# Two second-product tiles in a row: first products 3, 2, 0, 2 between the tiles of the expert stage

## The chip, the cores and the metric

The kernel runs on one core of a Trainium2 chip. The metric is device time of the whole program in microseconds (us); each time below is the median of three runs. TensorE (PE) does the matrix products, VectorE (DVE), ScalarE (ACT) and GpSimd (POOL) everything else; weights and tokens come and go by DMA, issued from SyncE (SP).

## What is computed

1152 tokens of 512 columns pass through three layers: a two-part attention (the first 170 us, with the first steps of the next layer beside it), a layer of 8 experts with a gate `P` that is balanced in 8 rounds (called the balancing below), and a dense layer with softplus.

```python
x = attention(q, k, v)                      # (1152, 512)
P = balanced(exp(x @ w_gate))               # 8 rounds of row and column sums
out = 0
for e in range(8):
    out += P[:, e:e+1] * (maximum(x @ w1[e], 0) @ w2[e])
h = out @ w_in
return softplus(h) @ w_out                  # d_ff = 2048
```

## The kernel before

**Tiling.** The tokens stand in two groups, s = 0 (512 tokens, four tiles of 128) and s = 1 (640 tokens, five tiles). The dense layer with its 2048 hidden columns is treated as two further "experts", e = 8 and 9, whose weights are brought into the same form earlier. An expert's hidden columns come in four pieces p. One *step* n of the list `steps` is one expert, one piece and one token group; there are 80, numbered from 0, and steps 4 to 79 are issued by the loop at the end of the kernel with an order fixed by hand on PE, ACT, DVE and POOL.

**First products.** `first(n)` makes the hidden values of step n. A fast matrix multiplication replaces eight products of half size by seven (`OPS = 7`). Each is six matmuls at L841: two halves of the contraction, times three pairs of high and low parts of the operands, with 256 columns for s = 0 and 320 for s = 1. They come in the order 4, 0, 2, 5, 1, 3, 6 and share three accumulators of PSUM, `m0`, `m1`, `m2`. Product 4 goes to an accumulator `m4` in the listings, and a copy `t1` of it is taken by ACT (`kept`, L853). Product 0 goes to `m0`, copied as `t5`. Product 2 is *added into the accumulator of product 4*, so its first matmul must wait until `t1` has been copied; the sum is copied as `u2`, and only then product 1 is written over it. Product 5 has the third accumulator. DVE adds the pieces (`combine`, L860): `c11` after product 5, `c22` after product 1, `c12` after product 3; `c21` is product 6 itself.

**Hidden values.** For each of the four pieces a job `hidden` is put into the planner. In the expert layer it is a ReLU on ACT (L778) and a subtraction on DVE (L780), giving high and low parts. In the dense layer it is a softplus chain of nine instructions: ACT Abs (L788), ACT Exp (L790), DVE +1 (L799), DVE error (L801), ACT Ln (L803), POOL subtraction (L805), DVE maximum and sum (L808), ACT cast (L810), DVE subtraction (L812). In the dense layer `c21` is also copied by ACT (L853) first.

**Second products.** `second` multiplies one tile of 128 tokens of hidden values with the second weights: six matmuls of 512 columns at L929. `weigh` adds the result to the output rows on DVE.

**The order on PE.** While step n makes its second products, tile by tile, the first products of a later step (usually n + 2) are issued between the tiles; `ahead` says which. Before each tile a share of what is left is issued, rounded up:

```python
for m, i in enumerate(tiles):
    for _ in range(-(-left // (len(tiles) - m))):
        next(products)
        left -= 1
```

With seven products this gives 2, 2, 2, 1 before the four tiles of an s = 0 step and 2, 2, 1, 1, 1 before the five of an s = 1 step. I call the tiles A, B, C, D and E in the order in which they are issued. During steps 4 to 8 one piece of the balancing follows every tile but the first; every second piece has a small matmul (L727) that needs what DVE made in the piece before.

**The order on the other engines.** The class `Order` is a planner with assumed durations. Every product and tile moves its clock on (`advance`), and it puts each waiting job instruction on its engine where it expects the engine free. ACT, DVE and POOL work their lists off in that order, so an instruction whose input is late holds up all those behind it. Where a step needs something of a job, `until` issues that job, and others with it. Besides the hidden chains the planner issues the splitting of weights, of the dense layer's weights (L351 to L375), and of the tokens between the layers (`operands`: L437 and L441 on DVE, L439 on ACT).

Of the kernel before, what the change touches and what calls it, by code (L numbers as in the profile page):

```python
# [20 lines left out]
def attention_moe_mlp(ctx: ExitStack, tc: tile.TileContext, q, k, v, w_gate, w1, w2, w_in, w_out, out):  # L21
# [3 lines left out]
    E, _, FF = w1.shape  # L25
# [26 lines left out]
    OPS = 7  # L52
# [654 lines left out]
    def sinkhorn():  # L707
        mt = spare[0][:, HALF[1] : HALF[1] + P]
        nc.tensor.transpose(mt[:1], m1, ident)
        m2 = const.tile([1, 1], F32, name="m2")  # L710
        nc.vector.tensor_reduce(m2, mt[:1], axis=AX.X, op=ALU.max)
        yield
        mb = spare[0][:, HALF[1] : HALF[1] + 1]
        nc.tensor.matmul(mb, ones[:1, :], m2, start=True, stop=True)
        m3 = const.tile([P, 1], F32, name="m3")
        nc.vector.tensor_copy(m3, mb)
        nc.vector.tensor_scalar(prf, prf, m3, None, op0=ALU.subtract)
        nc.scalar.activation(prf, prf, AF.Exp)
        for it in range(8):
            rs = const.tile([P, NTT, 1], F32, tag="grs", name="grs")  # L720
            nc.vector.tensor_reduce(rs, pr, axis=AX.X, op=ALU.add)
            nc.vector.tensor_scalar(rs, rs, EPS, None, op0=ALU.add)
            nc.vector.reciprocal(rs, rs)
            nc.vector.tensor_tensor(pr, pr, rs.to_broadcast([P, NTT, E]), op=ALU.mult)
            yield
            cp = spare[0][:, HALF[1] : HALF[1] + NTT * E]
            nc.tensor.matmul(cp, ones, prf, start=True, stop=True)  # L727
            cs = const.tile([P, 1, E], F32, tag="gcs", name="gcs")
            nc.vector.tensor_reduce(
                cs, cp.rearrange("p (t e) -> p e t", e=E), axis=AX.X, op=ALU.add  # L730
            )
            nc.vector.tensor_scalar(cs, cs, EPS, None, op0=ALU.add)
            nc.vector.reciprocal(cs, cs)
            nc.vector.scalar_tensor_tensor(
                out=pr, in0=pr, scalar=float(NT) / E, in1=cs.to_broadcast([P, NTT, E]), op0=ALU.mult, op1=ALU.mult
            )
            yield
# [14 lines left out]
    for e, g, s, p in steps:  # L752
        m = e * NP + p
# [161 lines left out]
    def outputs(s):  # L915
        return [bank(tag, "yps") for tag in ("at", "at", "at", "at", "y")[: len(TILES[s])]]

    def second(n, hh, hl, i, y, start, stop):
        s = steps[n][2]
        order_.force(fetching[uses[n], 1])  # L920
        for j, job in making[n]:
            if j * HALF[s] < (i + 1) * P and (j + 1) * HALF[s] > i * P:
                order_.force(job)
        wh, wl = weights[uses[n]][1]
        tok = slice(i * P, (i + 1) * P)
        m = 0
        for f in range(2):
            for a, b in ((hh, wh), (hh, wl), (hl, wh)):
                nc.tensor.matmul(y, a[:, f, tok], b[:, f, :], start=(start and m == 0), stop=(stop and m == 5))  # L929
                m += 1  # L930
        order_.advance(6 * 0.231)
# [6 lines left out]
    def scale_rows(t):  # L938
        yield "POOL", 0.95, order_.free.get("DVE", 0.0)
        nc.gpsimd.tensor_tensor(acc[t], acc[t], pr[:, t, 0:1].to_broadcast([P, DM]), op=ALU.mult)  # L940
# [3 lines left out]
    def weigh(e, s, i, y):  # L944
        t, e = TILES[s][i], min(e, E)
        once = (e, t) not in seen
        seen.add((e, t))
        if e in (0, E) and once:
            acc[t] = rows[s].tile([P, DM], F32, tag="row", name="acc")
            order_.did("DVE" if i % 2 else "ACT", 0.65)  # L950
            (nc.vector.tensor_copy if i % 2 else nc.scalar.copy)(acc[t], y)
        elif e in (0, E):
            order_.did("DVE", 0.745)
            nc.vector.tensor_tensor(acc[t], y, acc[t], op=ALU.add)
        else:
            if e == 1 and once:
                order_.force(scaled[t])
            order_.did("DVE", 0.745)
            nc.vector.scalar_tensor_tensor(  # L959
                out=acc[t], in0=y, scalar=pr[:, t, e : e + 1], in1=acc[t], op0=ALU.mult, op1=ALU.add,  # L960
            )

    def again(s, banks):

        if not s:
            order_.force(converting[0])
        if s:
            xf = [pair("xf2") for _ in range(2)]
        else:
            xf = [x.tile([P, 2, 2 * HALF[s]], F32, tag="raw", name="xf2") for x in rawp]  # L970
        for i, t in enumerate(TILES[s]):
            tp = bank(banks, "tp")
            for kk in range(KD):
                nc.tensor.transpose(tp[:, kk * P : (kk + 1) * P], acc[t][:, kk * P : (kk + 1) * P], ident)
            tpv = tp.rearrange("p (a k c) -> p a k c", a=2, k=2)
            order_.advance(0.43)
            for kk in range(2):
                order_.did("ACT", 0.38)
                nc.scalar.copy(xf[kk][:, :, i * P : (i + 1) * P], tpv[:, :, kk])
            yield  # L980
        for kk in range(2):
            split[s].append(order_.add(operands(s, kk, xf[kk], ORDER, [nc.vector], order_.free.get("ACT", 0.0)), 2, TURN))
# [7 lines left out]
    def used(n):  # L990
        f = uses[n]
        if final[f] == n and f + 3 < len(fetches):
            fetch_second(f + 3, fetches[f + 3])
# [93 lines left out]
    last = ends[E, 1]  # L1087
    ahead[last - 1], ahead[last] = [], [last + 1, last + 2]
    balance, pending = sinkhorn(), None

    def conversions():
        loaded = yield from load(pieces[0], 0.0)
        for piece, upcoming in zip(pieces, pieces[1:] + [None]):
            loaded = yield from convert(piece, *loaded, upcoming)
# [5 lines left out]
    def leading(ns):  # L1100
        for n in ns:
            if steps[n][0] == E and n == (turned[1] if steps[n][2] else ends[E, 1] + 1):
                for _ in pending:
                    pass
            yield from lead(n)

    engines = {mybir.EngineType.PE, mybir.EngineType.Activation, mybir.EngineType.DVE, mybir.EngineType.Pool}
    with tc.manual_schedule(engines=engines):
        order_.on = True
        order_.free.clear()  # L1110
        order_.read.clear()
        for n in range(BESIDE, len(steps)):
            if n == CV:
                converting.append(order_.add(conversions(), 2))
            e, g, s, p = steps[n]
            if begins[n]:
                ys = outputs(s)
            hs = ready.pop(n)
            products = leading(ahead.get(n, []))
            left = OPS * len(ahead.get(n, []))  # L1120
            if n == ends[E - 1, 0]:

                left -= len(TILES[0]) - 1

            half = [i for i in range(len(ys)) if (i + 1) * P > HALF[s]]
            half = half[1:] + half[:1] if HALF[s] % P else half
            tiles = half + [i for i in range(len(ys)) if i not in half]
            for m, i in enumerate(tiles):
                for _ in range(-(-left // (len(tiles) - m))):
                    next(products)  # L1130
                    left -= 1
                if pending:
                    next(pending, None)
                second(n, *hs, i, ys[i], begins[n], stops[n])
                if stops[n]:
                    weigh(e, s, i, ys[i])
                if m and balance:
                    order_.did("DVE", 0.6)
                    if next(balance, True):
                        balance = None  # L1140
                        for t in range(NTT):
                            scaled[t] = order_.add(scale_rows(t))
                if pending:
                    next(pending, None)
            if n == ends[E - 1, 0]:
                pending = again(0, "at")
                for _ in TILES[0]:
                    next(pending)
                    next(products, None)
            for _ in products:  # L1150
                pass
            used(n)
            if n == ends[E - 1, 1]:
                pending = again(1, "y")
            elif n in (ends[NE - 1, 0], ends[NE - 1, 1]):
                for t in TILES[s]:
                    nc.sync.dma_start(out[t * P : (t + 1) * P, :], acc[t])
# [25 lines left out]
```

## Time and profile before

| what | us |
|---|---|
| median of 3 runs | 1076.56 |
| lowest and highest run | 1076.06, 1077.1 |
| span of the profiled execution, first to last instruction | 1075.4 |
| PE busy in the span | 1052.5 (98%) |
| PE weight loads busy | 933.1 (87%) |
| DVE, ACT, POOL busy | 697.6 (65%), 567.0 (53%), 555.4 (52%) |
| matmuls of first products (L841), 3 x 1120 | about 1001 busy, overlapping |
| matmuls of second products (L929) with `hh`/`hl` and `h` | 502 x 3 and 436 + 218 |

The times of the runs include some 1.2 us that lie outside the profiled span. Matmuls are pipelined: one of 512 columns shows about 0.39 us of busy time, while the next one starts 0.23 us later. So the cost of a matmul is read from one start to the next, not from its busy time. The expert layer runs from about 170 us to 860 us, the dense layer with softplus from there to the end. I number products as in the code and write "first copy" for `t1`.

### The profile page before, as it was taken

What the parts mean: (1) busy time and instruction counts of PE and PEld (TensorE: products, weight loads), DVE (VectorE), ACT (ScalarE), POOL (GpSimd) and SP (SyncE); (2) the same over time, 40 slices, a digit from 0 to 9 for tenths busy, and PEclk for the clock granted to TensorE, in tenths of its full rate; (3) what the DMA queues carried; (4) which work ended last, traced back from release to release, by engine and by line L of the source; (5) the groups of instructions that cost most, each with busy time, mean ns of one, the idle gap of its engine ahead of it and who ended that gap; (6) DMA issues with size and microseconds to landing.
All of it is one profiled execution on the core that took longest, in us unless ns stands there. A gap on an engine that the chain in (4) does not pass through costs nothing.

```text
span 1075.4 us, 17729 instructions
## 1 busy us (share of the span) xinstructions
PE 1052.5 (98%) x6426; PEld 933.1 (87%) x6426; DVE 697.6 (65%) x1430; ACT 567.0 (53%) x1475; POOL 555.4 (52%) x575
## 2 busy tenths in 40 slices
PE   7989999999999999999999999999999999999998
PEld 4778888898989999898989989899998999788987
DVE  4797655776556566665656566565664678776765
ACT  3777634444444444454544444444454667676663
POOL 4556614477566566655566565664575412232221
PEclk8989989999999999999999999999999999999999
DMA  7654301222433334243333333343324373253112
GB/s 156 128 137 92 92 1 40 59 87 78 138 108 98 113 93 127 92 130 108 118 122 95 93 95 112 98 124 116 119 93 144 137 297 145 108 220 143 69 40 89
DMA packets 133495, 119.69 MB, mean 111 GB/s; under 512 B 35744, under 2 KB 111776, under 8 KB 133408
## 3 DMA queue, kind: packets, MB, share of 16 engines
q1 hardware_dynamic: 133408, 118.56, 36.1%
q8 instruction: 50, 0.82, 0.3%
q14 instruction: 37, 0.30, 0.1%
HBM read 93.11 MB, written 25.43 MB: 110 GB/s over the span
## 4 chain that ended last, share of the span: by engine, by line
PE 81%; DVE 10%; ACT 5%; POOL 1%; issue 1%; DMA 1%; SPq 1%; ACTq 0%; DVEq 0%
PE yps L929 40%; PE m L841 36%; DVE xl L441 2%; DVE ab L808 2%; POOL ab L805 1%; DVE ab L801 1%; ACT one L803 1%; PE sc L578 1%; DVE one L799 1%; ACT sc L590 1%; DVE c L860 1%; PE pv L637 1%; DVE hl L812 1%; PE tp L615 0%; DVE hl L780 0%
## 5 line engine op out<-in xcount | busy, mean ns | idle before, releaser
L841 PE MATMUL m<-xh,w1h 128*128 128x320 f32 (+1 forms) x1120 | 334.7, 299 | 2.8 <-DVE hl L780 1.6
L841 PE MATMUL m<-xl,w1h 128*128 128x320 f32 (+1 forms) x1120 | 333.3, 298 | 0.3 <-DVE xl L441 0.2
L841 PE MATMUL m<-xh,w1l 128*128 128x320 f32 (+1 forms) x1120 | 333.3, 298 | 0.0
L841 PEld LDWEIGHTS m<-xh,w1h 128*128 128x128 f32 x1120 | 213.1, 190 | 19.8 <-ACT t L853 2.8
L841 PEld LDWEIGHTS m<-xl,w1h 128*128 128x128 f32 x1120 | 213.1, 190 | 13.2 <-DVE xl L441 0.7
L841 PEld LDWEIGHTS m<-xh,w1l 128*128 128x128 f32 x1120 | 213.0, 190 | 0.4 <-POOL sums L244 0.2
L929 PE MATMUL yps<-w2h,hh 128*128 128x512 f32 x502 | 199.0, 396 | 2.2 <-ACT hh L810 2.2
L929 PE MATMUL yps<-w2l,hh 128*128 128x512 f32 x502 | 198.1, 395 | 0.0
L929 PE MATMUL yps<-w2h,hl 128*128 128x512 f32 x502 | 195.9, 390 | 0.0
L929 PE MATMUL yps<-w2h,h 128*128 128x512 f32 x436 | 153.0, 392 | 0.1
L295 POOL TENSOR_TENSOR w1l<-sums,w1h 128x512 fp32r<-128x512 f32 x72 | 99.2, 1389 | 88.7 <-ACT w1h L293 78.0
L860 DVE TENSOR_TENSOR c<-m,t 128x256 f32<-128x256 f32 (+1 forms) x160 | 72.7, 455 | 110.3 <-PE m L841 64.8
L316 POOL TENSOR_TENSOR w2l<-raw,w2h 128x512 fp32r<-128x512 f32 x72 | 98.4, 1385 | 59.8 <-ACT w2h L314 59.4
L805 POOL TENSOR_TENSOR ab<-one,ab 128x320 f32<-128x320 f32 (+1 forms) x64 | 54.6, 855 | 143.3 <-ACT one L803 143.3
L778 ACT ACTIVATE hh<-c 128x256 fp32r<-128x256 f32 (+1 forms) x138 | 61.0, 445 | 126.4 <-DVE c L860 126.2
L959 DVE SCALAR_TENSOR_TENSOR acc<-yps,pr,acc 128x512 f32<-128x512 f32 x117 | 87.3, 746 | 55.4 <-PE yps L929 54.7
L780 DVE SCALAR_TENSOR_TENSOR hl<-c,hh 128x256 fp32r<-128x256 f32 (+1 forms) x138 | 94.3, 687 | 33.0 <-ACT hh L778 31.4
L929 PEld LDWEIGHTS yps<-w2h,hl 128*128 128x128 f32 x502 | 94.3, 188 | 22.0 <-DVE hl L812 0.2
L929 PEld LDWEIGHTS yps<-w2h,hh 128*128 128x128 f32 x502 | 94.7, 189 | 15.2 <-ACT hh L810 2.6
L853 ACT COPY t<-m 128x256 f32<-128x256 f32 (+1 forms) x160 | 63.4, 398 | 78.4 <-PE m L841 78.2
L929 PEld LDWEIGHTS yps<-w2l,hh 128*128 128x128 f32 x502 | 94.8, 189 | 10.8
L929 PEld LDWEIGHTS yps<-w2h,h 128*128 128x128 f32 x436 | 82.0, 188 | 15.2 <-ACT h L810 0.3
(140 smaller groups left out, 1660.4 us busy)
## 6 DMA issues: line engine op xcount, KB each, us to landing
raw<-in_moe_w SPq DMA_DIRECT2D x72, 256.0 KB
raw<-in_moe_w SPq DMA_DIRECT2D x36, 512.0 KB
w1h<-s_in SPq DMA_DIRECT2D x10, 896.0 KB
w1l<-s_in SPq DMA_DIRECT2D x10, 896.0 KB
raw<-in_moe_w_in SPq DMA_DIRECT2D x32, 256.0 KB
raw<-in_moe_w_out SPq DMA_DIRECT2D x16, 512.0 KB
w2l<-s_out SPq DMA_DIRECT2D x10, 512.0 KB
w2h<-s_out SPq DMA_DIRECT2D x10, 512.0 KB
```

Source lines behind the costliest of these rows:

```text
L295: behind(chain, nc.gpsimd.tensor_tensor(lo[:, part], sums, hi[:, part].bitcast(F32), op=ALU.subtract))
L316: behind(chain, nc.gpsimd.tensor_tensor(lo[:, i], raw[:, i], hi[:, i].bitcast(F32), op=ALU.subtract))
L441: nc.vector.tensor_tensor(xl[s][:, i, kk], src, xh[s][:, i, kk].bitcast(F32), op=ALU.subtract)
L778: nc.scalar.activation(hh, c, AF.Relu)
L780: nc.vector.scalar_tensor_tensor(out=hl, in0=c, scalar=0.0, in1=hh.bitcast(F32), op0=ALU.max, op1=ALU.subtract)
L805: nc.gpsimd.tensor_tensor(ab, one, ab, op=ALU.subtract)
L808: nc.vector.scalar_tensor_tensor(out=ab, in0=c, scalar=0.0, in1=ab, op0=ALU.max, op1=ALU.add)
L841: nc.tensor.matmul(b[:, :h], x[:, i, kk, :], y[s][:, i, kk, :], start=(not more and n == 0), stop=(n == 5), skip_group_check=more,)
L853: nc.scalar.copy(t, b[:, :h])
L860: nc.vector.tensor_tensor(c, b[:, :h], t, op=ALU.add)
L929: nc.tensor.matmul(y, a[:, f, tok], b[:, f, :], start=(start and m == 0), stop=(stop and m == 5))
L959: nc.vector.scalar_tensor_tensor(out=acc[t], in0=y, scalar=pr[:, t, e : e + 1], in1=acc[t], op0=ALU.mult, op1=ALU.add,)
```

## The change

A step that issues exactly seven first products (69 of the 76 steps of the loop: 32 with four tiles, 37 with five) takes its shares from a table. Steps with none, with 14 or with fewer keep the old rule.

```diff
     balance, pending = sinkhorn(), None
+    SHARES = {4: (3, 2, 0, 2), 5: (3, 2, 0, 2, 0)}
...
             tiles = half + [i for i in range(len(ys)) if i not in half]
+            shares = SHARES[len(tiles)] if left == OPS else None
             for m, i in enumerate(tiles):
-                for _ in range(-(-left // (len(tiles) - m))):
+                for _ in range(shares[m] if shares else -(-left // (len(tiles) - m))):
                     next(products)
                     left -= 1
```

So a step reads on PE, products by their numbers:

| step | before | after |
|---|---|---|
| four tiles | 4 0, A, 2 5, B, 1 3, C, 6, D | 4 0 2, A, 5 1, B, C, 3 6, D |
| five tiles | 4 0, A, 2 5, B, 1, C, 3, D, 6, E | 4 0 2, A, 5 1, B, C, 3 6, D, E |

PE, in a four-tile step of the seventh expert, around tiles B and C (`yps_7871` and `yps_7868` before). `m4` is written here by product 1, `m0` by product 3. Before:

```order
L929 MATMUL yps_7871<-w2h_7368,h3_7660 128x512
L841 MATMUL m4_7872<-xh1_2069,w1h_7112 128x320
...
L841 MATMUL m4_7872<-xh1_2069,w1l_7113 128x320
L841 MATMUL m0_7885<-xh1_2069,w1h_7112 128x320
...
L841 MATMUL m0_7885<-xh1_2069,w1l_7113 128x320
L929 MATMUL yps_7868<-w2h_7368,h3_7659 128x512
```

The same place after, where B and C are `yps_7891` and `yps_7888`:

```order
L841 MATMUL m4_7892<-xh1_2069,w1l_7126 128x320
L929 MATMUL yps_7891<-w2h_7386,h3_7675 128x512
...
L929 MATMUL yps_7891<-w2h_7386,h3_7676 128x512
L929 MATMUL yps_7888<-w2h_7386,h3_7675 128x512
...
L929 MATMUL yps_7888<-w2h_7386,h3_7676 128x512
L841 MATMUL m0_7904<-xh1_2069,w1h_7125 128x320
```

Product 1 has moved ahead of B, product 3 behind C, and no product stands between the two tiles.

ACT, in the dense layer, around the first copy of step 73, from the copy of `c21` of step 72 on (`ab_10812` is the chain of `c12`, `ab_10838` that of `c21`, `ab_10799` that of `c22`; the Ln with `one_10825` belongs to `c12`, the one with `one_10851` to `c21`). Before:

```order
L853 COPY c21_10836<-m4_10720 128x256
L788 ACTIVATE ab_10838<-c21_10836 128x256
L803 ACTIVATE one_10825<-one_10825 128x256
L790 ACTIVATE ab_10838<-ab_10838 128x256
L810 CAST hh_10766<-ab_10799 128x256
L803 ACTIVATE one_10851<-one_10851 128x256
L853 COPY t1_10872<-m4_10862 128x256
L853 COPY t5_10883<-m0_10874 128x256
L810 CAST hh_10766<-ab_10812 128x256
```

After (`ab_10825` and `one_10846` are `c12`'s, `ab_10837` and `one_10866` are `c21`'s, `ab_10788` is `c22`'s):

```order
L810 CAST hh_10764<-ab_10788 128x256
L788 ACTIVATE ab_10825<-c12_10823 128x256
L853 COPY c21_10835<-m4_10719 128x256
L790 ACTIVATE ab_10825<-ab_10825 128x256
L788 ACTIVATE ab_10837<-c21_10835 128x256
L790 ACTIVATE ab_10837<-ab_10837 128x256
L803 ACTIVATE one_10846<-one_10846 128x256
L853 COPY t1_10869<-m4_10857 128x256
L803 ACTIVATE one_10866<-one_10866 128x256
L853 COPY t5_10881<-m0_10871 128x256
```

The first copy stood behind the Ln of `c21`; now it stands behind the Ln of `c12`, and the Ln of `c21` behind it. The chains of `c12` and `c21` run side by side.

DVE, in step 64 (the first of the dense layer), from `c22` of step 66 to `c12` of step 66. `xl0`, `x0` and `xf2` are the splitting of the tokens of group 0 for the dense layer. Before:

```order
L860 TENSOR_TENSOR c22_10042<-m4_9960,t5_9979 128x320
L812 TENSOR_TENSOR hl_9861<-ab_9920,hh_9860 128x320
L441 TENSOR_TENSOR xl0_104<-xf2_9883,xh0_103 128x256
L799 TENSOR_SCALAR one_10063<-ab_10018 128x320
L801 SCALAR_TENSOR_TENSOR ab_10018<-one_10063,ab_10018 128x320
L860 TENSOR_TENSOR c12_10068<-m0_9970,u2_10002 128x320
```

After, with 19 rows between the two combinations, of which 14 (one of them doubled) belong to the splitting:

```order
L860 TENSOR_TENSOR c22_10042<-m4_9960,t5_9979 128x320
L799 TENSOR_SCALAR one_10046<-ab_10018 128x320
L437 TENSOR_TENSOR x0_10041<-xf2_9883 128x256
L437 TENSOR_TENSOR x0_10040<-xf2_9884 128x256
L812 TENSOR_TENSOR hl_9861<-ab_9920,hh_9860 128x320
...
L808 SCALAR_TENSOR_TENSOR ab_9939<-c21_9937,ab_9939 128x320
L441 TENSOR_TENSOR xl0_104<-xf2_9883,xh0_103 128x256 x2
L441 TENSOR_TENSOR xl0_104<-xf2_9884,xh0_103 128x256
L812 TENSOR_TENSOR hl_9861<-ab_9939,hh_9860 128x320
L860 TENSOR_TENSOR c12_10099<-m0_9970,u2_9990 128x320
```

Most of the token splitting has moved from behind `c12` to in front of it.

## Rows read from the trace of the kernel before

**Rows 1.** Busy time by stage, columns as the second line names them.

```profile
core 0: us, PE busy (x) PEld busy (x) DVE busy (x) ACT busy (x) POOL busy (x), PEclk, DMA share, GB/s
200.00:860.00 660.00, 659.82 (x3847) 594.00 (x3847) 408.02 (x696) 311.13 (x686) 399.94 (x380) 1.00 0.35 109
920.00:986.00 66.00, 65.38 (x402) 57.88 (x401) 48.76 (x123) 46.23 (x129) 19.70 (x25) 1.00 0.43 162
```

**Rows 2.** PE timeline, expert layer: start us, us, engine, line, instruction.

```profile
300.65 0.28 PE L841 MATMUL m<-xh,w1h 128*128 128x256 f32 x1
...
301.36 0.40 PE L929 MATMUL yps<-w2h,hh 128*128 128x512 f32 x1
...
302.75 0.28 PE L841 MATMUL m<-xh,w1h 128*128 128x256 f32 x1
...
307.67 0.28 PE L841 MATMUL m<-xh,w1h 128*128 128x256 f32 x1
...
309.10 0.40 PE L929 MATMUL yps<-w2h,h 128*128 128x512 f32 x1
```

**Rows 3.** PE timeline: first matmuls of tiles one, two and six of a run.

```profile
816.16 0.39 PE L929 MATMUL yps<-w2h,h 128*128 128x512 f32 x1
...
817.55 0.39 PE L929 MATMUL yps<-w2h,hh 128*128 128x512 f32 x1
...
822.99 0.39 PE L929 MATMUL yps<-w2h,hh 128*128 128x512 f32 x1
```

**Rows 4.** Timeline of PE and DVE around two pieces of the balancing.

```profile
206.49 0.39 PE L929 MATMUL yps<-w2h,h 128*128 128x512 f32 x1
207.06 0.44 PE L727 MATMUL m<-pr,ones 128*128 128x72 f32 x2 [0.18 <-DVE pr L724]
```

**Rows 5.** Timeline where products 4, 0, 2 already stand together (step 67).

```profile
925.81 0.28 PE L841 MATMUL m<-xh,w1h 128*128 128x256 f32 x1
...
926.53 0.28 PE L841 MATMUL m<-xh,w1h 128*128 128x256 f32 x1
...
926.73 0.37 ACT L853 COPY t<-m 128x256 f32<-128x256 f32 x1 [0.83 <-PE m L841]
...
927.24 0.29 PE L841 MATMUL m<-xh,w1h 128*128 128x256 f32 x1
```

**Rows 6.** Timeline at a late first copy (step 77), ACT and PE.

```profile
1050.99 0.37 ACT L853 COPY t<-m 128x256 f32<-128x256 f32 x1
...
1051.41 0.38 PE L841 MATMUL m<-xh,w1h 128*128 128x256 f32 x1 [0.32 <-ACT t L853]
```

**Rows 7.** ACT timeline, expert layer: what stood before a late first copy.

```profile
459.25 0.68 ACT L360 ACTIVATE raw<-raw 128x512 f32<-128x512 f32 x1 [1.55 <-DVE cva L355]
```

**Rows 8.** Groups of the softplus chain by shape, 920 to 1060 us: busy, mean ns.

```profile
L805 POOL TENSOR_TENSOR ab<-one,ab 128x256 f32<-128x256 f32 x29 | 23.0, 794 | 55.9 <-ACT one L803 55.9
L808 DVE SCALAR_TENSOR_TENSOR ab<-c,ab 128x256 f32<-128x256 f32 x29 | 16.0, 555 | 12.8 <-POOL ab L805 12.8
L801 DVE SCALAR_TENSOR_TENSOR ab<-one,ab 128x256 f32<-128x256 f32 x30 | 12.7, 425 | 0.9
L799 DVE TENSOR_SCALAR one<-ab 128x256 f32<-128x256 f32 x31 | 8.9, 288 | 4.7 <-ACT ab L790 4.7
```

**Rows 9.** Timeline of the latest first copy (step 70, products of step 72).

```profile
965.80 1.00 DVE L808 SCALAR_TENSOR_TENSOR ab<-c,ab 128x256 f32<-128x256 f32 x1 [0.63 <-POOL ab L805]
...
966.23 0.40 PE L929 MATMUL yps<-w2h,h 128*128 128x512 f32 x1
...
967.56 0.42 ACT L803 ACTIVATE one<-one 128x256 f32<-128x256 f32 x1 [0.32 <-DVE ab L801]
...
967.89 0.63 ACT L853 COPY t<-m 128x256 f32<-128x256 f32 x2
...
968.29 0.39 PE L841 MATMUL m<-xh,w1h 128*128 128x256 f32 x1 [0.52 <-ACT t L853]
```

**Rows 10.** PE timeline: the longest wait of the dense layer.

```profile
918.79 0.50 PE L929 MATMUL yps<-w2h,hh 128*128 128x512 f32 x1 [2.16 <-ACT hh L810]
```

## The prediction

> **What bounds the kernel now.** I read the busy time by stages first, then the PE timeline start by start, then the waits of PE, and last what ACT and DVE did before those waits. In the expert layer PE is the bound: it is busy for 659.82 of 660 us at the full clock, while DVE has 408, ACT 311 and POOL 400 [rows 1]. Only the balancing made it wait there by more than 0.1 us. So the expert layer gets faster only if PE's own sequence does. From 860 us on the softplus chains raise ACT and DVE to 46 and 49 of 66 us [rows 1], and PE waits now and then for a first copy [rows 6, 9] or for hidden values [rows 10].
>
> **Part 1: tiles that stand together.** A tile behind a product takes 1.39 us (301.36 to 302.75) [rows 2], and so does the first tile of a run (816.16 to 817.55) [rows 3]. The five starts from 817.55 to 822.99 give four tiles in 5.44 us, 1.36 each [rows 3]. So a tile behind a tile saves 0.03 us. The price: a product behind a tile takes 0.71 us (300.65 to 301.36), while two in a row take 1.43 (307.67 to 309.10) [rows 2], so a product that no longer stands behind a tile costs about 0.01. A four-tile step goes from four runs of tiles to three: -0.03 + 0.01 = -0.02. A five-tile step goes from five to three: -0.04. That is 32 x 0.02 + 37 x 0.04 = 2.1 us. In the four five-tile steps of the balancing its matmuls stand behind B and D and break both pairs: 0.16 back. Sum -2.0. Both sizes are seen at one or two places only and are rounded to 0.01, so the bounds are -1.0 and -3.0.
>
> The row speaks against a rule here. The Trainium skill ("TensorE: Matmul & The Clock Gate", section "Wait — 56ns, not 53.3ns?") gives each back-to-back matmul its columns at 2.4 GHz plus a fixed cost of some 2.5 ns, whatever stands before it. By that, part 1 is worth nothing; the rows show two prices for the same tile, so I go by the rows and keep the rule as a rival.
>
> **Part 2: the balancing.** Twice a matmul of the balancing came after tile D and found its input late. At 206.49 the last matmul of the tile started, and the next at 207.06 [rows 4]: 0.57 instead of 0.23, so 0.34; the other place cost 0.13. In DVE's new order the second combination and both ReLU subtractions come before the balancing's pieces, so the piece behind C is done before D ends. I take -0.4 (bounds -0.5 and +0.5, the same wait once more).
>
> **Part 3: product 2 loses its cover in the expert layer.** Product 2 writes where the first copy reads. Before, product 0 and tile A (0.72 + 1.39 us) lay between; now product 0 alone. Where 4, 0, 2 already stand together, PE does not stop: product 0 starts at 926.53, the copy runs from 926.73 for 0.37, and product 2 starts at 927.24, on time [rows 5]. PE resumes 0.05 us behind the copy's end (1050.99 + 0.37 = 1051.36, then 1051.41) [rows 6], so 0.09 us are left; with 320 columns 0.20, by the same reckoning. A copy that is later than this stops PE. The copies are late where a weight conversion stands before them: at 459.25 ACT waited 1.55 us for DVE and then ran 0.68 [rows 7], and the copy came 0.25 us late. Of the 57 first copies of the expert layer's steps two would have stopped product 2, by 0.04 and 0.99 us. The new ACT order has a conversion directly ahead of 33 copies (35 before). I take +0.6 (0 to 2).
>
> **Part 4: product 2 in the dense layer.** Here 12 steps use the new table, and the chains are close to the copy. In step 70 the first copy started at 967.89, behind the Ln at 967.56, and product 2 at 968.29, although tile A had started at 966.23 [rows 9]. Without the tile product 2 would have been due at 966.23, so it would have waited 2.06 us. The last one, step 77, would have waited 1.87 [rows 6]; all twelve together 11.6 us, between these two and nothing. Today, with the tile, three of them wait, for 1.6 us in all with the slow restart.
>
> The new order changes what stands ahead of the copy: the Ln of `c12` instead of the Ln of `c21`. Product 3 ends one product (0.72) earlier than product 6. With the old latenesses less 0.72 the six four-tile steps would wait 2.8 us. The other way to get it is to walk the chain from the start of product 5, in a four-tile step with 256 columns. Durations are those of [rows 8, 9]; the next instruction of an engine starts some 0.33 us after the one before it, as at 967.56 and 967.89 [rows 9].
> - Products 5 and 1 end at 0.7 and 1.4; results are readable 0.2 later (926.53 to 926.73, [rows 5]). Combination, Abs, Exp, +1, error, Ln bring the Ln of `c11` to 3.4 and that of `c22` to 4.2.
> - The POOL subtractions follow at 3.5 and 4.5, 0.79 each or more, and end at 5.3.
> - The first L808 is held until the second subtraction ends, as at 965.80, where one took 1.00 against a mean of 0.56; both are done at 5.9.
> - `c12` is combined behind them and one subtraction: 6.8. Abs, Exp, +1, error and Ln, 0.29 to 0.43 each with `c21`'s in between, end at 9.0; the first copy runs from 8.9 to 9.3.
> - Product 5, 1, B, C, 3, 6, D, 4, 0 make product 2 due at 8.4. Wait 0.9 us.
>
> With 0.9 in three steps, 0.7 in two, 0.1 in one this gives 4.2; between 2.8 and 4.2 I take 3.5. In a five-tile step E stands between as well. The same walk gives 0 to 0.1 where the copy stands behind the Exp of `c21`, and 0.7 to 1.0 where a cast of `c12` stands before it (two of six): 1.8, of which I take 1.6. Sum +5.1, less the 1.6 that exists: **+3.5** (bounds -1.6, if every copy is on time, and +10, if all twelve stay as late as now).
>
> **Part 5: the start of the dense layer.** The longest wait, 2.2 us before 918.79 [rows 10], is for softplus values that lay behind the token splitting on DVE. In the new order most of the splitting is issued before `c12` of step 66, so these values come earlier and the wait goes. What is next late: `t5` and `u2` of step 67, behind ten ACT instructions, would hold product 1 by about 0.7 us; and product 0 of step 67 needs `c12` read, which 15 splitting instructions (0.34 apart) and five chain ones (0.4) delay by some 7 us against 8.2 of PE work: near nothing to 0.3. So -2.3 + 1.0 = -1.3 (bounds -2.4 and +1).
>
> **Sum.** -2.0 - 0.4 + 0.6 + 3.5 - 1.3 = +0.4 us. The profiled execution spans 1075.4 us and the median of the runs is 1076.56, 1.2 us more, outside the part that changes. So the span would be 1075.8 and the median 1077.0. About 0.2% (2.15 us) is what a measurement of this kernel can tell from no change, so this is "no change".
>
> **Rivals.**
> - *The copies are on time (faster).* The new order groups the chains in pairs; if their Ln comes before the copy is due, the twelve waits shrink to some 1.2 us in all. Then 1077.0 - 3.9 = 1073.1. For it: in five-tile steps the walk leaves the copy room, and E stands behind product 6. Against it: the held L808.
> - *The copies stay as late as now (slower).* Mechanism: ACT's list is in order, so a first copy behind an Ln or cast waits for DVE and POOL, and with no tile between 0 and 2 PE waits with it, in each of twelve steps anew, since a stopped PE delays the next chain by as much. In full 11.6 instead of 5.1: 1083.5. It decides from 6.8 us in all, 0.57 a step. For it: six of the twelve would wait 1.2 to 2.1 us as they are today.
> - *No gain from standing together.* The longer first tile might belong to the tile's change of operands and not to what stands before it. Then -2.0 falls away: 1079.0. By the rule of the Trainium skill above it would come to the same. Against it: inside the run the change of tile costs nothing [rows 3].
>
> **How the numbers follow.** Forecast 0.47, with a range of its own from 1074.4 to 1078.7; copies on time 0.25; as late as now 0.23; no gain 0.05. Faster by over 0.2% is the second case, 0.25; within 0.2% the first, 0.47; slower the last two, 0.28. The range 1072.6 to 1081.0 holds the forecast, most of the second case and the half of the third in which the latenesses shrink a little; some 0.08 lies below and 0.1 above.
>
> **What would show it.** Right: steps of the expert layer shorter by 0.02 (four tiles) and 0.04 (five tiles), with tiles C and E taking 1.36 us; PE waits in front of product 2 for `t1` that sum to about 5 us after 860 us and to under 2 before; no wait of 2 us in step 66. Wrong: tiles C and E at 1.39; stops for `t1` all through the expert layer, behind L360 or L293; no stops at all in the dense layer, or stops of over 1.5 us in each step; or a new stop for `c12` in front of product 0.

## The result

The changed kernel takes 1088.55 us (median of 4 runs, 1086.95 to 1089.42); the kernel before took 1076.31 us. The ratio is 1.0109, with a 95% interval from 1.0082 to 1.0136: **1.1% slower**. I had forecast no change, 1077.0 us in a range from 1072.6 to 1081.0, so forecast and range were both wrong.

The profiled execution spans 1086.5 us, against 1075.4. Waits of PE after the change, from 200 us on (line waiting, engine and line waited for, us in total, times, longest):

```profile
PE m L841 <- ACT t L853: 6.1, 11, 1.6
PE m L841 <- DVE c L860: 3.7, 2, 3.0
PE yps L929 <- POOL w2l L316: 1.0, 2, 0.7
PE yps L929 <- DVE hl L780: 0.8, 1, 0.8
PE tp L974 <- ACT xf L979: 0.7, 1, 0.7
PE m L841 <- DVE hl L780: 0.2, 1, 0.2
```

Only the first line is a wait that I had priced at more than 0.3 us; the second, for combinations, I had put at near nothing to 0.3. Before, the same view held 1.1 us for `t`, 0.2 us for the balancing and the 2.2 us of [rows 10]. For the stretch from 200 to 860 us, in the columns of [rows 1]:

```profile
200.00:860.00 660.00, 656.57 (x3819) 591.28 (x3818) 410.37 (x692) 302.85 (x683) 395.05 (x381) 1.00 0.36 109
```

PE was busy for 659.82 of 660 us before, 656.57 now: it waits in the expert layer too.

To place the loss I took from the PE timelines the starts of product 4 of the steps 5, 59 and 68, and of the last matmul. (From here on a step is named by the products that are made for it; the tiles that run beside them belong to the step two lower, except for steps 60 to 65, 68 and 69.) Everything ahead of step 5 is the same code in all kernels, and still took 156.6 to 160.9 us in different executions. So small effects are read from step 5 on. All in us, each row from the one execution that was profiled (for e1 the slowest of its four); the experiments are told below, the sign is the difference from before:

```
kernel           5 to 59       59 to 68      68 to end     5 to end
before           643.64        121.33        145.47        910.43
after            645.37 +1.73  128.08 +6.75  149.80 +4.33  923.25 +12.82
e1 expert        645.20 +1.56  128.61 +7.28  145.40 -0.07  919.21  +8.78
e2 dense         643.70 +0.06  121.27 -0.06  149.82 +4.35  914.80  +4.37
e3 between       643.64  0.00  125.82 +4.49  145.05 -0.42  914.51  +4.08
e4 cover         642.87 -0.77  128.45 +7.12  146.90 +1.43  918.22  +7.79
e5 cover expert  642.83 -0.81  120.95 -0.38  145.41 -0.06  909.20  -1.23
e6 cover 64      642.76 -0.88  121.18 -0.15  145.43 -0.04  909.38  -1.05
e7 longer plan   643.70 +0.06  152.95 +31.6  149.53 +4.06  946.18  +35.8
e8 old at 64     645.09 +1.45  126.31 +4.98  150.15 +4.68  921.54 +11.11
e9 until 48      644.48 +0.84  122.55 +1.22  145.45 -0.02  912.49  +2.06
e10 later        651.63 +7.99  122.68 +1.35  149.77 +4.30  924.07 +13.64
e11 cover best   641.86 -1.78  122.45 +1.12  145.42 -0.05  909.72  -0.71
```

So the change costs 1.7 us in the expert layer, 6.75 us between the layers and 4.3 us in the dense layer.

### The profile page after: what moved, and what is told of

Read it like the earlier page. It is cut to its first block, busy times and chain, and to the rows that moved or that the text cites. A ratio compares the mean times of both kernels' runs of the same rounds, so it can differ in the third digit from the quotient of the medians.

```text
span 1086.5 us, 17745 instructions
## 1 busy us (share of the span) xinstructions
PE 1051.8 (97%) x6426; PEld 934.4 (86%) x6426; DVE 708.5 (65%) x1430; ACT 559.3 (51%) x1475; POOL 547.6 (50%) x575
## 4 chain that ended last, share of the span: by engine, by line
PE 74%; DVE 11%; ACT 7%; POOL 3%; issue 2%; DMA 2%; SPq 1%; ACTq 0%; DVEq 0%; POOLq 0%
PE yps L929 36%; PE m L841 33%; DVE ab L808 1%; DVE xl L441 1%; POOL ab L805 1%; DVE c L860 1%; PE sc L578 1%; DVE ab L801 1%; ACT one L803 1%; DVE acc L959 1%; DVE one L799 1%; DVE hl L780 1%; ACT sc L590 1%; ACT ab L790 1%; ACT ab L788 1%
## 5 line engine op out<-in xcount | busy, mean ns | idle before, releaser
L929 PE MATMUL yps<-w2h,h 128*128 128x512 f32 x436 | 147.5, 392 | 0.0
L316 POOL TENSOR_TENSOR w2l<-raw,w2h 128x512 fp32r<-128x512 f32 x72 | 98.2, 1379 | 45.5 <-ACT w2h L314 45.4
```

What stands on the lines that cost most here:

```text
L316: behind(chain, nc.gpsimd.tensor_tensor(lo[:, i], raw[:, i], hi[:, i].bitcast(F32), op=ALU.subtract))
```

## Where the time went, place by place

**Expert layer: six stops of product 2.** Timeline at step 14, DVE, ACT and PE (start, us, instruction, in brackets the idle time ahead and what ended it):

```profile
267.40 1.33 DVE L355 SCALAR_TENSOR_TENSOR cva<-raw,cva 128x512 uint32<-128x512 uint32 x1
...
268.77 0.69 ACT L360 ACTIVATE raw<-raw 128x512 f32<-128x512 f32 x1 [1.43 <-DVE cva L355]
...
269.09 0.31 PE L841 MATMUL m<-xh,w1l 128*128 128x320 f32 x1
269.35 0.74 ACT L853 COPY t<-m 128x320 f32<-128x320 f32 x2
...
269.82 0.41 PE L841 MATMUL m<-xh,w1h 128*128 128x320 f32 x1 [0.42 <-ACT t L853]
```

Product 4 was done by 268.6, but the first copy started at 269.35: ACT's list has L360 ahead of it, and L360 waited until DVE had finished L355. The planner assumes 0.8 us for L355; here it took 1.33. (Of the 32 executions of L355 in this trace, 21 took 0.68 to 0.70 us, with at most a tenth of that beside a POOL instruction; 11 took 1.11 to 1.72, with two thirds or more beside one. Those at the four stops of this kind ran wholly beside POOL's L316.) Product 2 started 0.73 us after the last matmul of product 0 instead of 0.15, and the matmul behind it 0.25 later instead of 0.15. Steps 14, 22, 42 and 50 lose 0.67 us each in this way. Step 12 loses 0.27 behind another instruction of this kind (L293, which had waited 0.89 us for POOL). Step 53 loses 0.34 with no instruction ahead of the copy; why it starts late there stays open. Together 3.3 us.

**Between the layers, 1: split weights (1.5 us).** Step 59 is followed by a long run of tiles without products. SP's list (DMA issues) before, then after, and two tiles of that run after the change:

```profile
793.54 0.34 SPq L340 DMA_DIRECT2D raw<-in_moe_w_out  x1
794.89 0.34 SPq L387 DMA_DIRECT2D s_out<-first  x1
796.17 0.93 SPq L265 DMA_DIRECT2D raw<-in_moe_w  x2
```

```profile
801.65 0.33 SPq L340 DMA_DIRECT2D raw<-in_moe_w_out  x1
802.26 0.33 SPq L387 DMA_DIRECT2D s_out<-first  x1
802.68 1.11 SPq L265 DMA_DIRECT2D raw<-in_moe_w  x2
...
807.13 0.41 ACT L276 CAST w1h<-raw 128x256 fp32r<-128x256 f32 x1 [1.17 <-DMA raw<-in_moe_w]
...
816.88 2.86 POOL L316 TENSOR_TENSOR w2l<-raw,w2h 128x512 fp32r<-128x512 f32 x2 [0.64 <-ACT w2h L314]
...
818.56 0.50 PE L929 MATMUL yps<-w2l,hh 128*128 128x512 f32 x1 [0.69 <-POOL w2l L316]
...
819.80 0.50 PE L929 MATMUL yps<-w2l,hh 128*128 128x512 f32 x1 [0.28 <-POOL w2l L316]
```

The load of an expert weight (L265) stands on SP behind the load and the store (L340, L387) of a conversion of the dense weights. In the new order that conversion ends 7 to 8 us later, some half a step, so L265 is issued at 802.68 instead of 796.17, the splitting starts at 807.13, and everything that takes its turn behind it slips: the last L316 ends when PE has long asked for it. (POOL's first instruction on these weights, L244, waits 4.44 us for the load. Just ahead of L316, ACT's L314 also stands behind a ReLU that waits 1.78 us.)

**Between the layers, 2: transposes (1.0 us).** While step 61's products run, groups of four transposes (L974) stand ahead of and behind tiles A and B, and ahead of C. With B and C together, the four behind B and the four ahead of C adjoin:

```profile
845.40 0.60 PE L974 MATMUL tp<-ident,acc 128*128 128x128 f32 x4
...
846.74 0.66 PE L974 MATMUL tp<-ident,acc 128*128 128x128 f32 x4 [0.74 <-ACT xf L979]
...
846.03 0.65 ACT L979 COPY xf<-tp 128x256 f32<-128x256 f32 x2 [0.84 <-PE tp L974]
```

The second four wait until ACT has emptied the first four's bank. I had not looked at what else stands between two tiles.

**Between the layers, 3: `c12` of step 66 (3.3 us, and half clock behind it).** DVE and PE:

```profile
902.50 1.17 DVE L812 TENSOR_TENSOR hl<-ab,hh 128x320 fp32r<-128x320 f32 x1
903.60 0.48 DVE L860 TENSOR_TENSOR c<-m,t 128x320 f32<-128x320 f32 x1
...
911.40 0.48 DVE L860 TENSOR_TENSOR c<-m,u 128x320 f32<-128x320 f32 x1
...
899.74 0.39 PE L929 MATMUL yps<-w2h,h 128*128 128x512 f32 x1
...
904.13 0.41 PE L841 MATMUL m<-xh,w1h 128*128 128x320 f32 x1 [0.61 <-DVE c L860]
...
908.59 0.31 PE L841 MATMUL m<-xh,w1l 128*128 128x320 f32 x1
911.94 0.41 PE L841 MATMUL m<-xh,w1h 128*128 128x320 f32 x1 [3.04 <-DVE c L860]
```

The two combinations shown are `c22` (903.60) and `c12` (911.40). Product 1 was done when tile B started at 899.74, so `c22` itself ran some 3.7 us late, behind instructions of the chains and of the splitting; product 6, which writes where `c22` reads, waited 0.8 us for it. Between `c22` and `c12` stand 15 splitting instructions and five of the chains. `c12` is read 7.8 us after `c22`; PE has product 6, two tiles and product 4 to do meanwhile, 4.6 us (904.13 to 908.74), and product 0 of step 67 must not overwrite what `c12` reads. Behind the long wait the granted clock falls (columns: stretch, its length, PE busy, matmuls in brackets, clock, DMA):

```profile
904.20:908.60 4.40, 4.40 (x24) 1.00 0.00 0
912.00:916.00 4.00, 4.00 (x15) 0.57 0.01 5
916.00:920.00 4.00, 4.00 (x23) 1.00 0.00 0
```

A matmul of 320 columns takes 0.267 us there instead of 0.147, the lower of the two levels (1.2 GHz); 1.5 us in all. The 2.2 us wait of [rows 10] is gone, as predicted.

The rest of this stretch is one more late hidden value in front of a tile of step 62 at 866.77 (1.1 us), where the ReLUs of ACT and DVE stand among the token splitting.

**Dense layer.** Seven first copies stop product 2, by 0.41, 0.79 and 0.71 (steps 71 to 73), 0.44 and 0.48 (74, 75), 0.97 (77) and 1.77 us (79), each with a slow restart of 0.1. The last:

```profile
1060.39 0.42 ACT L803 ACTIVATE one<-one 128x256 f32<-128x256 f32 x1 [0.32 <-DVE ab L801]
1060.71 0.63 ACT L853 COPY t<-m 128x256 f32<-128x256 f32 x2
...
1061.12 0.39 PE L841 MATMUL m<-xh,w1h 128*128 128x256 f32 x1 [1.61 <-ACT t L853]
```

This is [rows 9] once more: the copy behind a Ln (L803), now with nothing on PE to cover it.

## The experiments

**One stretch at a time.** Three kernels use the new shares in one part of the steps only (`n` is the step whose tiles run):

```
-            shares = SHARES[len(tiles)] if left == OPS else None
+            shares = SHARES[len(tiles)] if left == OPS and n < 57 else None         (e1)
+            shares = SHARES[len(tiles)] if left == OPS and n > 65 else None         (e2)
+            shares = SHARES[len(tiles)] if left == OPS and 56 < n < 66 else None    (e3)
```

e1. 

> The new table only in steps n < 57 (the expert layer), the old rule behind them. Theory (the loss is made in three places that do not need each other): in the trace of after, from first products 5 to 58, six stops in front of product 2 cost 3.3 us with their slow restarts, the pairs and the balancing give 1.9 back: about 1077.5 us, within 0.2% of the kernel before, with the same four stops of about 0.57 us behind L360. Rival (a disturbance of the expert layer is carried on and grows behind it): at least half of the 12.2 us, so 1082 or more.

e2. 

> The new table only in steps n > 65 (the dense layer). Theory: from first product 4 of step 68 to the last matmul the trace of after lost 4.3 us on that of before, so about 1080.5 us, with seven stops in front of product 2 of 0.4 to 1.8 us. Rival (these stops come from the order between the layers being late): under 1078, and fewer than three stops.

e3. 

> The new table only in steps 57 to 65 (the end of the expert layer and the start of the dense one). Theory: the longest part of the loss, 6.7 us, arises here: about 1083 us, with the waits for split weights (0.85 and 0.45), for the transposes' copies (0.95), for c21 (0.8) and for c12 (3.2) and matmuls at 1.2 GHz behind the last. Rival: the late weights and c12 come from the planner's state that the expert layer leaves; then they are gone here and the time is under 1079.

Measured (ratios are to runs of the kernel before that were taken beside them): e1 1082.09 us (ratio 1.0069, 1.0043 to 1.0095), e2 1081.01 (1.0049, 1.0028 to 1.0071), e3 1081.10 (1.0056, 1.0035 to 1.0076). **e2** is as the theory says: +4.35 us behind step 68, nothing ahead of it, seven stops of product 2. The dense layer's loss needs nothing from elsewhere. **e3** loses 4.49 us in its own stretch, with the transposes and both waits for combinations (the one that the expectation calls `c21` is `c22`), but without the late weights:

```profile
PE m L841 <- DVE c L860: 3.6, 2, 3.0
PE m L841 <- ACT t L853: 1.3, 3, 0.5
PE tp L974 <- ACT xf L979: 0.7, 1, 0.7
```

So transposes and `c12` come from the new shares at their own place, and the late weights do not. **e1** refutes my theory that the three places are independent. Its expert layer costs +1.56, as expected, but it loses 7.28 us more between the layers, where it runs by the old rule:

```profile
PE m L841 <- ACT t L853: 3.8, 8, 0.8
PE yps L929 <- ACT hh L810: 2.2, 1, 2.2
PE yps L929 <- POOL w2l L316: 1.4, 3, 0.7
PE m L841 <- DVE hl L780: 1.3, 2, 0.9
```

On SP L265 is issued at 804.04 here, again behind L340 at 803.00. The rival was right in this point: the expert layer hands something on. The stretch 59 to 68 is not a sum of two parts, since after has 6.75 and e1 and e3 together 11.8.

**What is handed on: PE's delay, or the planner's order?**

```
+            shares = SHARES[len(tiles)] if left == OPS and n < 48 else None    (e9)
```

> Shares 3, 2, 0, 2 (and 0) in steps n < 48, the old rule behind them. On ACT the built order is that of the kernel before again from step 56 to 60. Theory (what the expert layer hands on is the planner's order of weight splitting and conversions, not PE's delay): the stops in front of product 2 stay in the first 48 steps, and between steps 59 and 68 nothing is lost against before (within 0.5 us), where the run with these shares for n < 57 lost 7.3 us. Rival (PE's delay is handed on): 3 to 7 us lost there again.

Measured: one run, 1079.06 us. The stops at steps 12, 14, 22 and 42 are there, and PE is 0.84 us late at step 59. L265 is issued at 796.85, nothing waits for split weights, and from step 59 to 67 the kernel gains 0.36 us on before. (The +1.22 up to step 68 is 1.6 us at half clock, told below.) In e1 that stretch loses 5.7 us; the other 1.6 of its 7.28 are half clock, as in e9. So what costs 5.7 us in e1 comes with the order that the planner makes when the shares change in steps 48 to 56. A delay of 0.84 us by itself costs nothing further on; e1's 1.56 was not tried alone.

**Is it the cover of product 2, or the pairs?**

```
-    SHARES = {4: (3, 2, 0, 2), 5: (3, 2, 0, 2, 0)}
+    SHARES = {4: (2, 3, 0, 2), 5: (2, 3, 0, 2, 0)}    (e4)
```

> Shares 2, 3, 0, 2 (and 0) in all 69 steps: the pairs stay, but tile A stands between product 0 and product 2 again. Theory (product 2 without cover costs 3.3 us in the expert layer and about 5 in the dense one, the rest of the loss has other causes): no stop over 0.2 us in the expert layer, 1080 to 1083 us. Rival (it is the pairs, through the hidden values that two tiles in a row need at once): 1086 or more, and waits in front of tiles in the expert layer.

Measured: 1082.92 us (1.0070, 1.0044 to 1.0096). The expert layer is 0.77 us shorter than before, with no stop of product 2; but two late copies `u2` stop product 1, at steps 21 and 26 (0.57 and 0.26 us), where I expected no stop over 0.2. In the dense layer the loss falls from 4.33 to 1.43 us: product 2 no longer stops, product 1 does, for `u2`, by 0.2 to 0.9 us. Between the layers 7.12 us remain, the largest part a wait of product 6 for `c22` of step 67:

```profile
PE m L841 <- DVE c L860: 5.0, 1, 5.0
PE m L841 <- ACT u L853: 2.4, 6, 0.8
PE tp L974 <- ACT xf L979: 0.7, 1, 0.7
```

In the expert layer and the dense layer the theory holds: the pairs pay, and what costs is the tile that was taken from between products 0 and 2. It does not explain the loss between the layers, which this cover leaves as large as it was. The 1080 to 1083 us were met, with a wait for `c22` in place of the one for `c12`.

**Cover for both copies.** B and C could also stand between products 5 and 1:

```
+    SHARES = {4: (2, 2, 0, 3), 5: (2, 2, 0, 3, 0)}    (e10, in all steps but 57 to 65)
```

> Shares 2, 2, 0, 3 (and 0) in all steps but 57 to 65: B and C stand together, but tile A is between products 0 and 2, and B and C between products 5 and 1, so that both the first copy and the copy u2 have cover. Theory (all new stops come from these two covers): no stop over 0.2 us in the expert layer, in the dense layer only those of the kernel before, and 1.5 to 2.5 us less than before from step 5 to the end: 1073 to 1075 us. Rival (products 1, 3 and 6 come a tile later, and with them c22, c12 and c21; tiles then wait for hidden values in the dense layer): over 3 us lost behind step 68, 1078 us or more.

Measured: 1088.96 us (1.0121, 1.0085 to 1.0156). Both expectations missed: the theory its time, the rival its mechanism, though 4.30 us were lost behind step 68 and 1078 us exceeded, as it said. Neither copy stops PE, and no tile newly waits for hidden values; instead product 6 stops behind products 1 and 3, 17 times:

```profile
PE m L841 <- DVE c L860: 10.0, 17, 1.6
PE yps L929 <- ACT hh L810: 2.2, 1, 2.2
```

```profile
577.62 0.47 DVE L860 TENSOR_TENSOR c<-m,t 128x320 f32<-128x320 f32 x1
...
578.15 0.42 PE L841 MATMUL m<-xh,w1h 128*128 128x320 f32 x1 [0.28 <-DVE c L860]
```

Products 1, 3 and 6 now stand together. DVE is behind with its combinations, and product 6 writes where `c22` reads, with product 3 alone as cover. Every tile between first products is some product's cover.

**L360 ahead of the copy.** The planner is told a longer time for L355; PE's order is that of the changed kernel:

```
-        t = yield "DVE", 0.8, t
+        t = yield "DVE", 1.4, t    (L355 only; e7)
```

> The changed kernel, with 1.4 instead of 0.8 us assumed by the planner for the DVE instruction L355, so that no L360 stands directly ahead of a first copy. Theory (an L360 that waits for L355 makes the copy late and stops product 2): the four stops of 0.57 us at steps 14, 22, 42 and 50 are gone, and from first product 4 of step 5 to that of step 58 the kernel needs 2 to 3 us less than the changed one, if no other conversion takes L360's place. Rival (the copy waits for something else, PSUM or product 4 itself): the four stops stay.

Measured: one run, 1112.27 us. The four stops at steps 14, 22, 42 and 50 are gone, and steps 5 to 58 take 1.67 us less than in the changed kernel (the expected 2 to 3 less what new, smaller stops take: seven of 0.23 to 0.64 us, six of them for `u2`). That confirms L360 as the cause of those four. But the conversions now end later, and the last ones still ran beside the dense layer:

```profile
902.48 0.43 DVE L353 TENSOR_SCALAR cva<-raw 128x512 uint32<-128x512 uint32 x1 [5.34 <-DMA s_out<-cva]
...
905.78 0.48 DVE L860 TENSOR_TENSOR c<-m,t 128x320 f32<-128x320 f32 x1
...
906.32 0.63 PE L841 MATMUL m<-xh,w1h 128*128 128x320 f32 x1 [14.32 <-DVE c L860]
```

A combination stood behind a conversion that waited for a DMA, and PE stood still for 14.5 us. One duration, changed by 0.6 us in the plan, cost 24.9 us between the layers against the changed kernel; two further waits for combinations, of 4.3 and 5.5 us, are in it.

**The old rule at 64 and 65 alone**, the rest as changed:

```
+            shares = SHARES[len(tiles)] if left == OPS and n not in (64, 65) else None    (e8)
```

> The changed kernel with the old rule in steps 64 and 65 alone. Theory (the token splitting that the new shares put ahead of c12 of step 66 on DVE stops product 0 of step 67): the waits of 0.8 and 3.2 us in front of product 6 of step 66 and product 0 of step 67 are gone, a wait of 2.3 us before a tile, as in the kernel before, is back: 1.5 to 3 us less than the changed kernel from step 66 to 68. Rival (the late chains come from the expert layer's order): product 0 of step 67 still waits over 1 us.

Measured: one run, 1084.05 us. Both waits for combinations are gone, and the wait of 2.3 us in front of a tile is back. From step 66 to 68 it takes 1.64 us less than the changed kernel, at the low end of the expectation, since matmuls at half clock followed this wait too.

**A version that keeps the gain.** Shares 2, 3, 0, 2 (and 0) without the places that cost:

```
+            shares = SHARES[len(tiles)] if left == OPS and n < 57 else None                         (e5)
+            shares = SHARES[len(tiles)] if left == OPS and n < 64 and n != 60 else None             (e6)
+            shares = SHARES[len(tiles)] if left == OPS and n < 57 and n not in (19, 24) else None   (e11)
```

e5. 

> Shares 2, 3, 0, 2 (and 0) in steps n < 57, the old rule behind them. Theory: with tile A between products 0 and 2 the expert layer is 0.8 us shorter from first product 4 of step 5 to that of step 59 (as in the run with these shares everywhere), and no split weights come late behind it, since product 2 never stops PE and the planner's order of weights fits: 0.5 to 2 us faster than before in the trace from step 5 to the end, about 1075 us. Rival (any new order of the expert layer leaves the planner with split weights and tokens that come late, as with shares 3, 2, 0, 2): 5 to 7 us lost between steps 59 and 68, about 1081 us.

e6. 

> Shares 2, 3, 0, 2 (and 0) in steps n < 64 without step 60, the old rule elsewhere. Theory: as the run with them for n < 57, 0.2 us less for five more pairs; the wait of 0.95 us at the transposes between the layers, which came with a pair of tiles in step 60, is gone: about 1075 us. Rival (the transposes' copies are late because of what ACT does, not because eight transposes stand together): the 0.95 us stays.

e11. 

> Shares 2, 3, 0, 2 (and 0) in steps n < 57 without 19 and 24, the old rule elsewhere. In the run with all steps below 57 two late copies u2 stopped product 1 of steps 21 and 26, for 0.53 and 0.25 us and a slow restart each. Theory (the pairs and the balancing are all that the table is worth, and every stop is local): both stops gone, 2.0 to 2.3 us less than before from step 5 to the end, about 0.2% faster, at the limit of what the times can tell. Rival (the stops move to other steps): 1.0 to 1.5 us less, not to be told from no change.

Measured: e5 1075.73 us (1.0005, 0.9987 to 1.0023), e6 1075.01 (1.0000, 0.9986 to 1.0014), e11 1075.31 (0.9995, 0.9976 to 1.0015). None can be told from the kernel before by its time. In the traces, from step 5 on, they take 1.23, 1.05 and 0.71 us less (for e11 I expected 2.0 to 2.3). The rival of e5, 5 to 7 us lost between steps 59 and 68, did not come. In e6 the transposes do not wait, so it is their adjoining that costs 0.95. In e11 both stops are gone, 1.78 us are gained up to step 59, as the theory says, and no stop has moved elsewhere in the expert layer; 1.5 us at half clock took most of it back.

## Why the prediction was wrong, point by point

- **Part 1, pairs: right.** Two tiles together take 2.74 us (first matmul at 522.05, next product at 524.79), 1.39 + 1.36 as taken from [rows 2, 3]:

```profile
522.05 0.39 PE L929 MATMUL yps<-w2h,h 128*128 128x512 f32 x1
...
524.79 0.30 PE L841 MATMUL m<-xh,w1h 128*128 128x320 f32 x1
```

  Undisturbed steps are 0.02 and 0.03 to 0.04 us shorter each. The rival "no gain from standing together" is refuted. The Trainium skill ("TensorE: Matmul & The Clock Gate", section "Wait — 56ns, not 53.3ns?") gives a warm matmul one fixed cost beside its columns; by that both tiles would cost the same, and the trace does not agree: 1.39 and 1.36 us.
- **Part 2, balancing: right.** Its two waits are gone; the steps there are 0.36 and 0.13 us shorter, -0.5 where I took -0.4.
- **Part 3, product 2 in the expert layer: failed**, +3.3 instead of +0.6, beyond its bound of 2. I took how late the copies would have been from the old trace, though the order of ACT's list was about to change, and [rows 7] had shown the mechanism: L360 waiting 1.55 us for L355. The new order put an L360 that was not ready ahead of four copies that have 0.2 us to spare. I had counted conversions ahead of copies (33 against 35), but not asked which of them would wait.
- **Part 4, dense layer: nearly right.** The stretch gave +4.33, with its pairs' gain of some 0.3 in it; I took +3.5, and the bounds hold it. New stops sum to 5.6 us and 0.7 for restarts, where I took 5.1. The four-tile steps gave 3.3 (taken: 3.5); the five-tile steps gave 3.0, where I took 1.6, since I gave the last step no more than the others and it stops for 1.77 us. Neither rival happened: "as late as now" priced the stops at 11.6, "on time" at 1.2.
- **Part 5, start of the dense layer: failed**, +3.1 from step 66 to 68 instead of -1.3. The mechanism was named: the splitting instructions delay `c12`, which product 0 of step 67 needs read. The delay was nearly right, too: I took 7 us, and it is 7.8. Wrong was where it begins. The 8.2 us of PE work are those from the end of product 1 to product 0 (four tiles and products 3, 6 and 4), as if `c22` ran when product 1 was done; I had read DVE's list from `c22` on and put its own lateness at nothing. It ran 3.7 us late, when tiles B and C and product 3 were over, and from product 6, which waited for it, to product 0 only 4.6 us were left. The stop of 3.2 us was then followed by the half clock (1.5 us), which the sum has no term for. The 0.7 that I took for product 1 of step 67 did not come.
- **Missing from the sum: steps 59 to 66, +3.65 us**: split weights 1.5, transposes 1.0, hidden values 1.1. For a change of order I had checked the instructions around the moved products, but not the transposes that stand beside every tile there, nor SP's list, where a weight load stands behind another job's store.

Sum of the pieces: +1.73, +3.65, +3.11 and +4.33 give 12.82 us; the part of the program ahead of step 5 happened to be 1.76 us quicker in the execution that was profiled, hence the span's 11.1. Between this and the forecast of +0.4 lie 12.4 us. Part 5 and the steps ahead of it are 8 of them, Part 3 is 2.7, Part 4 some 1.

What stays open: why the planner, given other shares in steps 48 to 56, puts the last conversions half a step later. That it does is seen on SP and in e9; which of its rules tips I did not follow.

## What to carry to other kernels

A tile between two products that share an accumulator is that accumulator's cover; before moving it, list for every first product what must be read before it writes, and the engine and the list in which this reading stands. Where a planner fills the other engines' lists, a change of PE's order is a change of all lists: compare the built order of each engine, SP's included, at every change of stage, and price a moved reading as (its new delay) less (the PE work left in between), both counted from the same instruction. A gain of 0.03 us a step on PE is smaller than one stop.

## What the runs showed of the hardware

Of the kernels in which PE waits 2.3 us in front of a tile (as in [rows 10]), four had the full clock behind it (before, e2, e5, e6) and five ran at 1.2 GHz for a while (e1, e8, e9, e10, e11), at a price of 1.5 to 1.6 us. In the traces of e5 and e11 the instructions follow in the same order from long before this place (on PE from 420 us on, on ACT from 628, on DVE from 801, on POOL from 835), and the wait is 2.32 and 2.31 us. The 4 us behind it, e5 and then e11:

```profile
916.40:920.40 4.00, 4.00 (x18) 1.00 0.25 97
```

```profile
913.50:917.50 4.00, 4.00 (x13) 0.61 0.28 110
```

So with one and the same order the clock may fall behind such a wait or not, and with it 1.5 us come or go. Behind the longer waits, of 3.2 us (the changed kernel and e3) and 5.2 us (e4), it fell each time. The Trainium skill ("TensorE: Matmul & The Clock Gate", section "What's actually happening") says that the gate looks at windows that run freely and are not started by the kernel, so that the point of change moves from run to run; this pair, one execution each, agrees with it.
